# Adding C21 in place in PSUM, moving attention steps inside the periods, and another passage from the second to the third batch

## The chip, the cores and the metric

The kernel runs on 1 core of one Trainium2 chip. The metric is the device time of one execution in microseconds (us); lower is better. The engines are named as in the profile: PE (TensorE, matmuls; PEld its weight loads), DVE (VectorE), ACT (ScalarE), POOL (GpSimd) and SP (SyncE, which here only issues DMAs).

## The reference

Attention in two steps, then a gated feed-forward layer, in float32:

```python
def _attn_ref(q, k, v, p):                 # q, k, v: (8, 8, 576, 64); p: (8, 8, 32, 64)
    scale = 1.0 / np.sqrt(q.shape[-1])
    def sm_attn(qq, kk, vv):
        s = scale * np.matmul(qq, kk.transpose(0, 1, 3, 2))
        s = s - np.max(s, axis=-1, keepdims=True)
        a = np.exp(s)
        a = a / (np.sum(a, axis=-1, keepdims=True) + 1e-09)
        return np.matmul(a, vv)
    p_packed = sm_attn(p, k, v)            # 32 packed rows look at 576 keys
    return sm_attn(q, p_packed, p_packed)  # 576 rows look at the 32 packed rows

def _moe_ref(x, w_a, w_b, w_out):          # x: (4608, 512), w_a and w_b: (512, 1536), w_out: (1536, 512)
    return ((x @ w_a) * (x @ w_b) @ w_out).astype(np.float32)
```

`x` is the attention's output with the heads laid side by side: 8 batches of 576 rows.

## The kernel before

The kernel goes batch by batch (b = 0 to 7). `p_packed` is never multiplied into x. It is folded into the weights: for each batch and each of 12 column tiles `ft` of w_a and w_b, PE computes G = p_packed times the weights, and then a = A2 G, where A2 is the second attention's softmax. Every float32 product is made of three matmuls in a rounded format: the operand is split into a high part (a cast on ACT) and a low part (source minus high part: `lo_part`, L91, on POOL or DVE), and hi x hi, hi x lo and lo x hi are summed in PSUM. The last product (h times w_out, "mm2") is made in thirds of four `ft` each, tile of 128 rows by tile.

**Batches 0 and 1** multiply plainly (`mm1`, L383). After each half of an `ft` the function `between()` emits the steps written down for that slot in a string, `PLAN`, for the work on the next batch: 24 slots in the 12 `ft`, then one for each call of a loop in which PE makes 6 matmuls of mm2 per slot. What stands behind a ";" is emitted at the next making of G.

**Batches 2 to 7** save one product in eight by a scheme of seven products per `ft` (numbered 1 to 7 in `PRODUCTS`) on halves of 288 rows; two of their sums are kept apart as `d` and `c2` (C21). Each `ft` is a *period*, n = 0 to 71, and works on two `ft` at once: it ends tile n and begins tile n+1, in two pairs of PSUM banks, X and V, one bank of each for even and one for odd tiles. A period runs so:

- even n: `make_g(n + 2)`: PE L777 makes G for two tiles from weights `wr` that a DMA has brought (one buffer, asked for by `load_kept` as soon as the last pair has been read); ACT copies it (`gs`, L783, L785, L786); DVE and POOL make sums of its quarters (L788, L789, L792).
- products 5, 1 and 2; ACT copies X to `d` (L829); `split_h` casts the h of the period before (ACT L808) and POOL takes its low part; PE fills in mm2 matmuls (L720) as `FILLS` says; DVE adds V to `d` (L833).
- products 3 and 6, for which that copy must be done; ACT copies X to `c2` (L841); `split_g` casts a G tile (ACT L798) and POOL takes its low part; DVE makes the second half of h from X and `d` (L846).
- fill; products 4 and 7; DVE adds V to `c2` (L856) and multiplies by the `d` of the period before (L857); fill.

Between these parts `emit_steps` emits steps of the next batch's attention. Steps are names: "S0", "S1" begin the first attention for even and odd heads and "r0", "r1" go one yield further in it (`stage1`); "s0", "s1" go further in the second one (`stage2`: matmuls, a DVE transpose and maximum, a subtraction on POOL L323, the exponential on ACT L325, sums L328 to L330 on DVE, a product on POOL L331, a transpose on DVE L335); "P" and "T" turn a small tile on PE and copy it (`turned`, L242); "k" and "q" turn a loaded block on DVE (L124); "L.." issue DMAs on SP; "t" forms four differences of the softmax halves on POOL (`half_sums`, L598); "u0" to "u3" cast these to high parts on ACT (L612) and make their low parts on DVE (`half_parts`).

From L564 on the order is the order of the source on each engine: every engine works its own queue first in, first out, and an instruction that waits holds all behind it.

The **passage** from the second to the third batch: after the last `mm1`, PE has 96 matmuls of mm2 to fill in: 24 in the loop of slots, 36 in each of the periods n = -2 and n = -1, which start the scheme. Before the change all four `half_parts` stand between the loop and period -2:

```python
    for i in range(4):
        half_parts(NB, i)
```

Of the kernel before, what the change touches and what calls it, by code (L numbers as in the profile page):

```python
# [12 lines left out]
ALU = mybir.AluOpType  # L13
AX = mybir.AxisListType.X
# [5 lines left out]
def tile_packed_attn_gated_ffn(  # L20
# [35 lines left out]
    NB = 2  # L56
# [179 lines left out]
    def turned(dst, src, back=0):  # L236

        tp = bank_pair(True)[:, 0, :] if paired[0] else bank()
        cols = src.rearrange("p e d -> p (e d)")
        for i in range(2):  # L240
            nc.tensor.transpose(tp[:, P * i:P * i + P], cols[:, 64 * (i ^ back):64 * (i ^ back) + P], ident)
        nc.vector.tensor_copy(out=dst.rearrange("p i r j -> p (i r j)"), in_=tp[:, 0:2 * P])  # L242

    pp, paired, a2f_of = {}, [False], {}

    def stage1(b, e):
# [13 lines left out]
        nc.vector.tensor_reduce(out=nmx, in_=s, axis=AXY, op=ALU.max)  # L260
        nc.vector.tensor_scalar(out=nmx, in0=nmx, scalar1=-scale, scalar2=None, op0=ALU.mult)
        a1 = work(b, f"a1_{e}", [P, S], "t1")
        rs = sm.tile([P, 1], F32, name="rs")
# [43 lines left out]
    def stage2(b, e):  # L307
# [9 lines left out]
        s2 = work(b, f"s2_{e}", [P, TU, J], "t1")  # L317
        nc.vector.transpose(out=s2.rearrange("p (u x) j -> p u (x j)", u=2), in_=x[:, :, 0:HS])
        mx = sm.tile([P, TU], F32, name="mx")
        nc.vector.tensor_reduce(out=mx, in_=s2, axis=AX, op=ALU.max)  # L320
# [6 lines left out]
        sum2 = sm.tile([P, TU], F32, name="sum2")  # L327
        nc.vector.tensor_reduce(out=sum2, in_=s2, axis=AX, op=ALU.add)  # L328
        nc.vector.tensor_scalar(out=sum2, in0=sum2, scalar1=1e-9, scalar2=None, op0=ALU.add)
        nc.vector.reciprocal(out=sum2, in_=sum2)  # L330
# [121 lines left out]
    def emit(b, plan, tasks={}):  # L452

        for name in plan.split():
# [44 lines left out]

    PLAN = (" |  |  | S0 | r0 | r0 |  | r0 |  | r0 Lv1 ; S1 | r1 | q0 Lk2 | r1 | r1 |  | r1 q1 Lk3 Lv2 P0 |  | T2 | "  # L500
            "s0 s0 Lp4 | s0 s1 | s1 s0 | s0 s1 | s1 | s0 s1 k2 | s1 t | k3 | Lq2")
    PLAN = dict(enumerate(PLAN.split("|")))
# [113 lines left out]
    def emit_steps(b, steps):  # L616

        for name in steps.split():
            if name in "ABCD":
                emit(0, name)  # L620
            elif b >= B:
                continue
            elif name == "t":
                half_sums(b)
            elif name[0] == "u":
                half_parts(b, int(name[1]))
            else:
                emit(b, name)
# [126 lines left out]

    banks_of = {}

    def product(n, k, bank, first):
# [52 lines left out]
    def period(n, fills, steps):  # L811
# [5 lines left out]
        both = slice(0 if here and k0 == 0 or there and k1 == 0 else 1, 2 if here and k0 == 1 or there and k1 == 1 else 1)  # L817
        emit_steps(b + 1, steps[0])
        if more and n % 2 == 0:
            make_g(n + 2)  # L820
        emit_steps(b + 1, steps[1])
        if here:
# [4 lines left out]
        if here or there:  # L827
            d = d_of[n] = lp.tile([P, 2, HS], F32, name="d", bufs=2)
            nc.scalar.copy(out=d[:, both], in_=X[:, both, 0:HS])  # L829
        split_h(n - 1)  # L830
        fill(fills[0])
        if here or there:
            nc.vector.tensor_tensor(out=d[:, both], in0=V[:, both, 0:HS], in1=d[:, both], op=ALU.add)  # L833
        flush()
        emit_steps(b + 1, steps[2])
        if here:
            product(n, 3, X, False)
        if there:
            product(n + 1, 6, X, False)
            c2 = c2_of[n + 1] = lp.tile([P, HS], F32, name="c2", bufs=2)  # L840
            nc.scalar.copy(out=c2, in_=X[:, k1, 0:HS])  # L841
        if more:
            split_g(n + 2)
        if here:
            hf = hf_of[n] = sm.tile([P, 2, HS], F32, name="asb")
            nc.vector.tensor_tensor(out=hf[:, 1], in0=X[:, k0, 0:HS], in1=d[:, k0], op=ALU.mult)  # L846
        fill(fills[1])
        flush()
        emit_steps(b + 1, steps[3])
        if here:  # L850
# [3 lines left out]
        if here:  # L854
            c2 = c2_of.pop(n)
            nc.vector.tensor_tensor(out=c2, in0=V[:, k0, 0:HS], in1=c2, op=ALU.add)  # L856
            nc.vector.tensor_tensor(out=hf[:, 0], in0=d_of.pop(n - 1)[:, k0], in1=c2, op=ALU.mult)  # L857
        fill(fills[2])
        flush()
        emit_steps(b + 1, steps[4])  # L860

# [8 lines left out]
    filler[0] = block()  # L870
    while slot[0] <= max(plan) or (slot[0] - start) % 2:
        fill(6)
        flush()
        between()
    for i in range(4):
        half_parts(NB, i)
    STEPS = {0: ("S0", "", "r0", "r0 Lq1", "Lv1"), 1: ("", "", "r0", "", ""), 2: ("r0", "S1", "r1", "r1", ""),
# [65 lines left out]
```

## Time and profile before

| | |
|---|---|
| median of 3 runs | 739.31 us (738.4 to 740.46) |
| profiled execution, its own time | 738.6 us |
| its span, first to last instruction | 736.8 us |
| PE busy | 707.6 us (96%) |
| DVE, ACT, POOL busy | 474.8, 359.9, 424.6 us |
| mean granted PE clock | 0.995 |
| first period of batch 2; end of the last | about 207 us; about 714 us |

Read it so: PE is busy nearly always, so a change can only shorten the time by what PE still waits, or by the time in which it runs at a lower clock; the other engines count where PE waits for one of them. A row of a timeline is: start, duration, engine, line, operation, output <- input, shape, count, and in brackets the idle time of that engine before it and what ended it.

### The profile page before, as it was taken

The numbers are of one execution on the slowest core, as the hardware profiler recorded it, in microseconds if no ns is written. First come the engines' busy times: TensorE is split into PE (matmuls) and PEld (weight loads), VectorE is DVE, ScalarE is ACT, GpSimd is POOL, SyncE is SP. The second block draws the span as 40 slices with busy tenths as digits, with TensorE's granted clock in tenths as the row PEclk, the third lists the DMA queues.
The fourth block names the chain that finished last, engine by engine and source line by source line (L and its number), as shares of the span: only waits on it lengthen the run. The fifth ranks groups of instructions, "written<-read, shape, count | busy, mean of one in ns | idle before, by whom it ended". The sixth has DMA issues, their size and how long they took to land.

```text
span 736.8 us, 14156 instructions
## 1 busy us (share of the span) xinstructions
PE 707.6 (96%) x5558; PEld 574.3 (78%) x5558; DVE 474.8 (64%) x828; ACT 359.9 (49%) x724; POOL 424.6 (58%) x322
## 2 busy tenths in 40 slices
PE   6899999998899999999999999999999999999998
PEld 4488878886787876888788877778778887788886
DVE  3888655557255769676786668776686576755442
ACT  3787744543334455544554355553555445545420
POOL 0586752336234678656775568656685567856530
PEclk9999999999899999999999999999999999999999
DMA  8999954576234733555354564347235422224002
GB/s 253 381 248 293 256 102 90 180 196 214 68 90 141 175 120 90 157 156 142 109 118 116 139 171 112 90 135 195 87 90 143 138 86 70 102 79 151 1 1 72
DMA packets 177059, 102.37 MB, mean 139 GB/s; under 512 B 141280, under 2 KB 159456, under 8 KB 171616
## 3 DMA queue, kind: packets, MB, share of 16 engines
q1 hardware_dynamic: 176992, 101.47, 48.4%
q8 instruction: 43, 0.70, 0.4%
q14 instruction: 24, 0.20, 0.1%
HBM read 85.72 MB, written 15.73 MB: 138 GB/s over the span
## 4 chain that ended last, share of the span: by engine, by line
PE 75%; POOL 9%; DVE 5%; ACT 3%; DMA 3%; issue 3%; SPq 1%; DVEq 0%; POOLq 0%; ACTq 0%
PE x L720 30%; PE m L763 21%; PE m L383 8%; PE m L409 5%; PE x L777 4%; POOL G_lo L91 3%; DMA wr<-w_kept 2%; POOL h_lo L91 2%; POOL t L323 1%; PE s L298 1%; PE s L254 1%; PE s L313 1%; POOL t L331 1%; PE x L365 1%; ACT gs L783 1%
## 5 line engine op out<-in xcount | busy, mean ns | idle before, releaser
L720 PE MATMUL x<-wo,h_hi 128*128 128x512 f32 (+1 forms) x776 | 242.6, 392 | 5.9 <-ACT gs L783 5.6
L91 POOL TENSOR_TENSOR h_lo<-asb,h_hi 128x576 fp32r<-128x576 f32 x96 | 141.7, 1476 | 114.7 <-ACT h_hi L808 58.9
L720 PEld LDWEIGHTS x<-wo,h_hi 128*128 128x128 f32 x776 | 139.0, 189 | 27.2 <-ACT gs L783 8.0
L720 PE MATMUL x<-wo,h_lo 128*128 128x512 f32 (+1 forms) x388 | 152.1, 392 | 0.0
L91 POOL TENSOR_TENSOR G_lo<-gs,G_hi 128x640 fp32r<-128x640 f32 x72 | 114.2, 1586 | 47.5 <-ACT G_hi L798 47.5
L720 PEld LDWEIGHTS x<-wo,h_lo 128*128 128x128 f32 x388 | 73.2, 189 | 13.6
L833 DVE TENSOR_TENSOR d<-m,d 128x576 f32<-128x576 f32 (+1 forms) x73 | 54.3, 744 | 44.4 <-ACT d L829 44.2
L91 POOL TENSOR_TENSOR A_lo<-gs,A_hi 128x256 fp32r<-128x256 f32 x36 | 27.8, 773 | 77.3 <-ACT A_hi L786 77.3
L829 ACT COPY d<-m 128x576 f32<-128x576 f32 (+1 forms) x73 | 46.5, 637 | 52.0 <-PE m L763 35.2
L730 DVE TENSOR_TENSOR part<-x,part 128x512 f32<-128x512 f32 (+1 forms) x65 | 44.1, 679 | 36.3 <-PE x L720 36.2
L763 PE MATMUL m<-tx_hi,G_lo 128*128 128x288 f32 x216 | 63.8, 296 | 0.8 <-POOL G_lo L91 0.8
L763 PE MATMUL m<-tx_hi,G_hi 128*128 128x288 f32 x216 | 64.5, 299 | 0.0
L763 PE MATMUL m<-tx_lo,G_hi 128*128 128x288 f32 x216 | 63.5, 294 | 1.0 <-DVE tx_lo L91 1.0
L783 ACT COPY gs<-x 128x512 f32<-128x512 f32 x36 | 21.1, 587 | 87.7 <-PE x L777 73.0
L846 DVE TENSOR_TENSOR asb<-m,d 128x288 f32<-128x288 f32 x72 | 32.3, 449 | 45.4 <-ACT c L841 43.1
L763 PEld LDWEIGHTS m<-a_hi,G_hi 128*128 128x128 f32 x144 | 27.0, 187 | 43.7 <-issue 18.2
L857 DVE TENSOR_TENSOR asb<-d,c 128x288 f32<-128x288 f32 x72 | 58.0, 805 | 2.5
L798 ACT CAST G_hi<-gs 128x640 fp32r<-128x640 f32 x72 | 52.8, 733 | 13.0 <-POOL gs L792 13.0
L841 ACT COPY c<-m 128x288 f32<-128x288 f32 x72 | 28.8, 400 | 52.8 <-PE m L763 52.2
L763 PE MATMUL m<-a_hi,G_hi 128*128 128x288 f32 x144 | 48.7, 338 | 6.1 <-ACT d L829 6.0
L808 ACT CAST h_hi<-asb 128x576 fp32r<-128x576 f32 x72 | 49.3, 684 | 5.2 <-DVE asb L857 5.2
L792 POOL TENSOR_TENSOR gs<-gs 128x512 f32<-128x512 f32 x36 | 46.7, 1296 | 0.1
(169 smaller groups left out, 1560.2 us busy)
## 6 DMA issues: line engine op xcount, KB each, us to landing
wr<-w_kept SPq DMA_DIRECT2D x36, 1024.0 KB
nat<-in_k_dram SPq DMA_DIRECT2D x56, 144.0 KB
nat<-in_q_dram SPq DMA_DIRECT2D x56, 144.0 KB
vt<-in_v_dram SPq DMA_DIRECT2D x28, 256.0 KB
out_dram<-part SPq DMA_DIRECT2D x27, 256.0 KB
raw<-in_moe_w_a_dram SPq DMA_DIRECT2D x12, 512.0 KB
raw<-in_moe_w_b_dram SPq DMA_DIRECT2D x12, 512.0 KB
raw<-in_moe_w_out_dram SPq DMA_DIRECT2D x12, 512.0 KB
```

The costliest lines, as they stand in the source:

```text
L91: return eng.tensor_tensor(out=dst, in0=src, in1=hi.bitcast(F32), op=ALU.subtract)
L383: nc.tensor.matmul(out=ps[:, half, 0:HS], lhsT=gt[:, kt, ft % 4, cols], rhs=at[:, kt, HS * half:HS * half + HS], start=(n == 0 and kt == 0 ...
L409: nc.tensor.matmul(out=o[:, cols], lhsT=ht[:, c0:c0 + P], rhs=wt[:, cols], start=(ft == 0 and n == 0), stop=(ft == NFT - 1 and n == 2))
L720: nc.tensor.matmul(out=o[:, cols], lhsT=ht[:, c0:c0 + P], rhs=wt[:, cols], start=(ft == fts[0] and n == 0), stop=end)
L730: nc.vector.tensor_tensor(out=parts[i][:, cols], in0=o[:, cols], in1=parts[i][:, cols], op=ALU.add)
L763: nc.tensor.matmul(out=bank[:, n % 2, 0:HS], lhsT=g, rhs=t, start=(first and i == 0), stop=(i == 2), skip_group_check=True)
L792: nc.gpsimd.tensor_tensor(out=gs[:, 2:4].rearrange("p a u f -> p a (u f)"), in0=gs[:, 0:2].rearrange("p a u f -> p a (u f)"), in1=s2.unsqu ...
L798: nc.scalar.copy(out=G_hi[:, n % 3], in_=gs[:, 1:6, n % 2])
L808: nc.scalar.copy(out=view(h_hi[ft]), in_=src)
L829: nc.scalar.copy(out=d[:, both], in_=X[:, both, 0:HS])
L833: nc.vector.tensor_tensor(out=d[:, both], in0=V[:, both, 0:HS], in1=d[:, both], op=ALU.add)
L857: nc.vector.tensor_tensor(out=hf[:, 0], in0=d_of.pop(n - 1)[:, k0], in1=c2, op=ALU.mult)
```

## The change

It adds and removes no arithmetic. In words:

1. `c2` is added to V in place in PSUM (L856 writes V, no longer `c2`), and the product behind it (L857) reads V from PSUM and `d` from SBUF, where both of its inputs were in SBUF.
2. For batches 3 to 7 the row sums of the second softmax are written to 18 free columns of X's banks and read from there (L328, L329).
3. `stage1` and `stage2` get one more yield each for batches 3 to 7, so that maximum and exponential, and transpose and maximum, can stand at different places.
4. In odd periods `split_g` stands at the period's start, ahead of the copy to `d`; in even ones where it was. `split_h` stands after the first fill, no longer before it.
5. The steps of the attention are given new places (`STEPS`, with places named pre, post, a, b, c, end).
6. In the passage, the steps of the third batch's attention go further in earlier slots of `PLAN`; "u0" and "u1" stand in its slots 24 and 26, "u2" and "u3" inside period -2.
7. The copies of "P" and "T" go to ACT, from the passage on.

```diff
-        nc.vector.tensor_copy(out=dst.rearrange("p i r j -> p (i r j)"), in_=tp[:, 0:2 * P])
+        copy = nc.scalar.copy if paired[0] else nc.vector.tensor_copy
+        copy(out=dst.rearrange("p i r j -> p (i r j)"), in_=tp[:, 0:2 * P])
...
         nc.vector.tensor_scalar(out=nmx, in0=nmx, scalar1=-scale, scalar2=None, op0=ALU.mult)
+        if b > NB:
+            yield
...
         nc.vector.transpose(out=s2.rearrange("p (u x) j -> p u (x j)", u=2), in_=x[:, :, 0:HS])
+        if b > NB:
+            yield
...
-        nc.vector.tensor_reduce(out=sum2, in_=s2, axis=AX, op=ALU.add)
-        nc.vector.tensor_scalar(out=sum2, in0=sum2, scalar1=1e-9, scalar2=None, op0=ALU.add)
+        total = banks_of["x"][:, e, HS:HS + TU] if b > NB else sum2
+        nc.vector.tensor_reduce(out=total, in_=s2, axis=AX, op=ALU.add)
+        nc.vector.tensor_scalar(out=sum2, in0=total, scalar1=1e-9, scalar2=None, op0=ALU.add)
...
-    PLAN = (" |  |  | S0 | r0 | r0 |  | r0 |  | r0 Lv1 ; S1 | r1 | q0 Lk2 | r1 | r1 |  | r1 q1 Lk3 Lv2 P0 |  | T2 | "
-            "s0 s0 Lp4 | s0 s1 | s1 s0 | s0 s1 | s1 | s0 s1 k2 | s1 t | k3 | Lq2")
+    PLAN = (" |  |  | S0 | r0 | r0 |  | r0 |  | r0 Lv1 ; S1 | r1 | r1 q0 Lk2 | r1 | r1 | q1 Lk3 Lv2 P0 |  ; s0 | s0 s0 | s0 T2 | "
+            "s0 Lp4 | s0 s1 | s1 s1 | s1 | s1 | s1 | t u0 | k2 | u1 | k3 Lq2")
...
-        emit_steps(b + 1, steps[0])
+        step = lambda at: emit_steps(b + 1, steps.get(at, ""))
+        step("pre")
         if more and n % 2 == 0:
             make_g(n + 2)
-        emit_steps(b + 1, steps[1])
+        elif more:
+            split_g(n + 2)
+        step("post")
...                                         # products 5, 1, 2; the copy to d
-        split_h(n - 1)
         fill(fills[0])
...                                         # the sum d
         flush()
-        emit_steps(b + 1, steps[2])
+        step("a")
+        split_h(n - 1)
...                                         # products 3, 6; the copy to c2
-        if more:
+        if more and n % 2 == 0:
             split_g(n + 2)
...                                         # the second half of h (L846)
+        step("b")
         fill(fills[1])
         flush()
-        emit_steps(b + 1, steps[3])
+        step("c")
...                                         # products 4, 7
             c2 = c2_of.pop(n)
-            nc.vector.tensor_tensor(out=c2, in0=V[:, k0, 0:HS], in1=c2, op=ALU.add)
-            nc.vector.tensor_tensor(out=hf[:, 0], in0=d_of.pop(n - 1)[:, k0], in1=c2, op=ALU.mult)
+            v = V[:, k0, 0:HS]
+            nc.vector.tensor_tensor(out=v, in0=v, in1=c2, op=ALU.add)
+            nc.vector.tensor_tensor(out=hf[:, 0], in0=v, in1=d_of.pop(n - 1)[:, k0], op=ALU.mult)
         fill(fills[2])
         flush()
-        emit_steps(b + 1, steps[4])
+        step("end")
...
-    while slot[0] <= max(plan) or (slot[0] - start) % 2:
+    while slot[0] <= max(plan) or (slot[0] - start) % 4:
         fill(6)
         flush()
         between()
-    for i in range(4):
-        half_parts(NB, i)
-    STEPS = {0: ("S0", "", "r0", "r0 Lq1", "Lv1"), 1: ("", "", "r0", "", ""), 2: ("r0", "S1", "r1", "r1", ""),
-             3: ("", "", "q0 r1", "", "Lk2"), 4: ("r1", "", "", "P0", ""), 5: ("", "", "q1", "T2", "Lv2 Lk3 Lp4"),
-             6: ("s0", "", "s0", "s0", "s0"), 7: ("", "", "s0", "s0", ""), 8: ("s1", "", "s1", "s1", "s1"),
-             9: ("", "", "s1 k2", "s1", "t"), 10: ("", "", "u0", "k3", "u1"), 11: ("", "", "u2", "", "u3 Lq2")}
+    STEPS = {-2: {"a": "u2", "c": "u3"}, 0: {"pre": "S0", "c": "Lq1", "end": "r0 Lv1"}, 1: {"a": "r0", "b": "r0 r0"},
+             2: {"pre": "r0", "post": "S1", "end": "r1"}, 3: {"a": "r1", "b": "r1 r1", "c": "q0", "end": "Lk2"},
+             4: {"pre": "r1", "c": "P0", "end": "q1"}, 5: {"b": "T2", "end": "Lv2 Lk3 Lp4"},
+             6: {"pre": "s0", "a": "s0", "end": "s0 s0"}, 7: {"a": "s0", "c": "s0", "end": "s0"},
+             8: {"pre": "s1", "a": "s1", "end": "s1 s1 k2"}, 9: {"a": "s1", "c": "s1", "end": "s1 t"},
+             10: {"a": "u0", "end": "u1"}, 11: {"a": "k3", "c": "u2", "end": "u3 Lq2"}}
...
-        period(n, (12, 12, 12), ("",) * 5)
+        period(n, (12, 12, 12), STEPS.get(n, {}))
```

More of the change, by code (lines that the diff above doesn't have):

```diff
@@ L241, in turned @@
             nc.tensor.transpose(tp[:, P * i:P * i + P], cols[:, 64 * (i ^ back):64 * (i ^ back) + P], ident)
-        nc.vector.tensor_copy(out=dst.rearrange("p i r j -> p (i r j)"), in_=tp[:, 0:2 * P])
-    pp, paired, a2f_of = {}, [False], {}
+        copy = nc.scalar.copy if paired[0] else nc.vector.tensor_copy
+        copy(out=dst.rearrange("p i r j -> p (i r j)"), in_=tp[:, 0:2 * P])
+    pp, paired, a2f_of, banks_of = {}, [False], {}, {}
     def stage1(b, e):
@@ L754, in fill @@
             next(filler[0], None)
-    banks_of = {}
     def product(n, k, bank, first):
```

## The prediction

> **What bounds the kernel now.** I read the page's busy times first, then stretches cut at the copies to `d`, so that each is one batch of 12 periods (2 to 6, then 7), then the chain of waits and the timelines where PE stood.
>
> ```profile
> PE 707.6 (96%) x5558; PEld 574.3 (78%) x5558; DVE 474.8 (64%) x828; ACT 359.9 (49%) x724; POOL 424.6 (58%) x322
> ...
> 209.30:295.50 86.20, 83.60 (x665) 67.71 (x665) 62.00 (x111) 42.16 (x90) 55.85 (x43) 1.00 0.49 132
> 295.50:381.50 86.00, 85.24 (x676) 69.78 (x675) 61.31 (x111) 43.27 (x92) 57.36 (x44) 1.00 0.47 129
> 381.50:468.20 86.70, 83.94 (x664) 67.37 (x664) 62.08 (x111) 42.74 (x91) 57.29 (x44) 1.00 0.49 131
> 468.20:554.30 86.10, 85.35 (x676) 69.86 (x675) 61.41 (x111) 43.35 (x92) 57.36 (x44) 1.00 0.47 128
> 554.30:639.40 85.10, 82.47 (x646) 66.87 (x645) 58.94 (x108) 42.67 (x91) 57.47 (x44) 1.00 0.33 104
> 639.40:709.20 69.80, 69.80 (x443) 59.34 (x442) 36.48 (x66) 31.26 (x62) 41.30 (x31) 1.00 0.20 76
> ```
>
> Columns: stretch, length, busy PE, PEld, DVE, ACT, POOL, PE clock, DMA. PE stands 2.60, 0.76, 2.76, 0.75 and 2.63 us in the five batches that carry attention for the next one, together 9.5, and nothing in the last. So the periods can give 9.5 us at most. Even batches lose more.
>
> The passage:
>
> ```profile
> 179.20:186.60 7.40, 1.85 (x17) 0.31 (x16) 6.94 (x10) 3.55 (x9) 4.54 (x6) 0.76 0.67 135
> 186.60:190.30 3.70, 3.69 (x10) 2.95 (x11) 1.54 (x5) 0.53 (x2) 1.99 (x2) 0.56 0.42 173
> ...
> 162.58 1.60 PE m L383 x12
> ...
> 179.70 1.35 PE L777 MATMUL x<-wr,ppT 64*32 64x512 f32 x12
> 186.61 1.22 PE L720 MATMUL x<-wo,h_hi 128*128 128x512 f32 x2 [5.55 <-ACT gs L783]
> ...
> 179.64 1.16 POOL L331 TENSOR_TENSOR t<-t,sum 128x576 f32<-128x576 f32 x1 [0.41 <-DVE sum L330]
> 181.75 0.79 POOL L598 TENSOR_TENSOR tf<-t,t 128x288 f32<-128x288 f32 x1 [0.95 <-DVE t L335]
> 183.49 0.88 POOL L598 TENSOR_TENSOR tf<-t,t 128x288 f32<-128x288 f32 x1
> 184.40 0.67 ACT L612 CAST tx_hi<-tf 128x576 fp32r<-128x576 f32 x1 [2.33 <-POOL tf L598]
> 185.98 0.57 ACT L783 COPY gs<-x 128x512 f32<-128x512 f32 x1
> ```
>
> PE stands 5.55 us: the bank that its next mm2 tile wants is free only after the copy to `gs`, which waits in ACT's queue behind the casts of `half_parts`, these for POOL's third difference, the differences for the softmax. Then the clock is low: 3.70 us at 0.56 are 3.70 x 0.44 = 1.6 us lost. Passage: 7.2 us. All PE loss that this change touches is 9.5 + 7.2 = 16.7 us; 739.3 - 16.7 = 722.6 is the floor.
>
> **The change part by part.**
>
> *Passage.* In the new slots stage 2 of the even heads is emitted three slots earlier, of the odd heads one, and nothing of it stands behind the even heads' product. A slot is 12 matmuls of `mm1`, 1.60 us in the chain's row. My estimate, walked through the queues: the odd heads' product (L331), now ahead of the last h's low part and free of the even heads', comes one slot earlier by its place and about two more by what no longer stands before it on POOL and DVE, at about 174.3 to 175.5 instead of 179.64; behind it the transpose on DVE (by 176.3) and the last low part on POOL, and the differences start at about 177.2 instead of 181.75. The first three took 184.40 - 181.75 = 2.65, so u1's cast ends about 180.5. A copy of an mm2 tile (as the `gs` copy, 0.57) stands behind it and frees the bank of the second half of G: 181.1, then `gs`: 181.7. PE resumes near 181.8 instead of 186.61: 4.8 us gained, a wait of some 2 us left. Ends: only one slot gained, 1.6; the whole wait gone, 5.55. u2 and u3 in period -2 lie beside 36 filler matmuls; if one came late, product 5 or 3 of period 0 would wait.
>
> The clock: PE's last matmul ended at 181.05. A mean of 0.76 over 7.40 us is 7.40 x 0.24 / 0.5 = 3.55 us at half clock, so it fell near 183.05, 2.0 us into the wait. I take it that it now stays up, since G's matmuls end later in the wait than before: gain 1.6, with 0 as the other end. The Trainium skill, "TensorE: Matmul & The Clock Gate", section "HAM oscillation — how this bites in real kernels", asks for no idle gap over about 3.4 us; by that rule the clock stays up and the sum stands. The trace saw it fall sooner, and by that the 1.6 us would be lost again: 727.6.
>
> *Exponential ahead of the copy to `d`.* Before, it is emitted at the end of periods 6 and 8:
>
> ```profile
> 272.43 1.37 POOL L323 TENSOR_TENSOR t<-t,mx 128x576 f32<-128x576 f32 x1
> ...
> 273.83 0.68 ACT L325 ACTIVATE t<-t 128x576 f32<-128x576 f32 x1 [1.61 <-POOL t L323]
> 274.42 0.62 ACT L829 COPY d<-m 128x576 f32<-128x576 f32 x1
> ...
> 275.10 0.40 PE L763 MATMUL m<-a_hi,G_hi 128*128 128x288 f32 x1 [0.92 <-ACT d L829]
> ...
> PE m L763 <- ACT d L829: 6.0, 10, 0.9
> ACT t L325 <- POOL t L323: 20.5, 13, 3.5
> ACT d L829 <- PE m L763: 35.2, 20, 3.3
> ACT gs L783 <- POOL G_lo L91: 14.7, 7, 2.1
> ```
>
> ACT waits for POOL's subtraction with the copy to `d` queued behind, and PE behind that. Now the exponential stands at "a" of periods 7 and 9, after the copy. The subtraction comes no sooner (POOL's queue ahead of it is the same), but only h's cast and `c2` stand behind it. These waits go: about 0.9 + 0.6 in an even batch, 0.6 in an odd. The sums, at "c", and the product then end about half a period later, but the odd-period `split_g` no longer stands before the differences. That early `split_g` also ends the 14.7 us that `gs` waited for G's low part. Its cast now precedes the copy to `d`, where ACT mostly idles for PE (35.2 us, 20 times): nothing. If that cover is gone it costs up to its 0.73 us (below).
>
> *C21.*
>
> ```profile
> L857 DVE TENSOR_TENSOR asb<-d,c 128x288 f32<-128x288 f32 x72 | 58.0, 805 | 2.5
> L846 DVE TENSOR_TENSOR asb<-m,d 128x288 f32<-128x288 f32 x72 | 32.3, 449 | 45.4 <-ACT c L841 43.1 <-issue 1.6 <-POOL h_lo L91 0.5
> L856 DVE TENSOR_TENSOR c<-m,c 128x288 f32<-128x288 f32 x72 | 32.2, 448 | 13.9 <-PE m L763 11.4
> ...
> L857 DVE TENSOR_TENSOR asb<-d,c x72: 457/602/1542, 214.4 to 714.8; 128x288 f32<-128x288 f32 x72
> L329 DVE TENSOR_SCALAR sum<-sum 128x18 f32<-128x18 f32 x16 | 10.0, 625 | 0.5
> ```
>
> L857 takes the form of L846: 805 - 449 = 0.36 us less, x 72 = 25.6 us of DVE. No row shows DVE writing PSUM: L856 stays at 448 by its own row, between 0.40 and 0.81 (the span of these rows). V is held through L857 too, 0.45 us longer: its next write is product 2 of the next period, at least products 7, 5 and 1 later, so hidden unless DVE is late by more than about 1 us. The ten sums of batches 3 to 7 drop by at most 0.6 each. All this is DVE time with PE busy elsewhere: nothing on the path but what follows.
>
> *Periods 10 and 11 of even batches.*
>
> ```profile
> 280.18 1.10 POOL L598 TENSOR_TENSOR tf<-t,t 128x288 f32<-128x288 f32 x1
> 285.01 1.29 POOL L792 TENSOR_TENSOR gs<-gs 128x512 f32<-128x512 f32 x1
> ...
> 284.74 1.36 DVE L124 STREAM_TRANSPOSE xT<-nat 128x1152 f32<-128x1152 f32 x1
> 288.54 1.51 DVE L91 TENSOR_TENSOR tx_lo<-tf,tx_hi 128x576 fp32r<-128x576 f32 x1
> ...
> 286.34 0.73 ACT L798 CAST G_hi<-gs 128x640 fp32r<-128x640 f32 x1 [2.78 <-POOL gs L792]
> 286.97 0.67 ACT L612 CAST tx_hi<-tf 128x576 fp32r<-128x576 f32 x1
> 288.10 0.64 ACT L829 COPY d<-m 128x576 f32<-128x576 f32 x1 [0.46 <-DVE asb L857]
> ...
> 290.10 0.40 PE L763 MATMUL m<-tx_lo,G_hi 128*128 128x288 f32 x1 [0.51 <-DVE tx_lo L91]
> ```
>
> Before, "k3" (1.36) and a long L857 push `tx_lo` to 288.54 and PE to 290.10. "k3" is now a period later and L857 short. What is late next is POOL: differences from about 279.6, L792 done by 285.4, then on ACT 0.73 + 0.67 + the next G's cast 0.73 before the copy to `d`: done about 288.2, PE's product 6 about 288.7. So 1.4 us are gained here, and a wait of about 1 us stays. With 0.6 from period 7 an even batch gains 2.0, an odd 0.75 (all it loses): 3 x 2.0 + 2 x 0.75 = 7.5. Ends: 2.0 in all (POOL's chain as late as now) and 9.5.
>
> *DMA.* No load is added.
>
> ```profile
> 430.87 8.45 SPq L700 DMA_DIRECT2D wr<-w_kept  x2
> ...
> 437.75 1.09 PE L777 MATMUL x<-wr,ppT 64*32 64x512 f32 x16 [0.47 <-DMA wr<-w_kept]
> ```
>
> This `wr` queues on SP behind the loads of period 5, which keep their place, and lands 6.9 us after its issue. Where PE comes 0.6 sooner it waits as much longer: -0.6 in batch 4 alone. The two copies per batch that go to ACT (busy 43 of 86 us) and the extra yields cost nothing; without ACT's slack a copy would hold what is behind it some 0.4 us.
>
> *Sum.* 4.8 + 1.6 + 7.5 - 0.6 = 13.3. The profiled execution took 738.6 (span 736.8 and 1.8 around it): 725.3. The median of the three is 0.7 higher: 726.0. I say 726.
>
> **The rivals.**
> 1. *POOL keeps the periods.* POOL is busy 56 of 86 us and its order around the differences hardly changes; with `split_g`'s cast in front the copy to `d` in period 11 is no earlier. Then the periods give 2.0: 739.3 - 6.4 + 0.6 - 2.0 = 731.5. Against: L857 and "k3" leave DVE's queue there.
> 2. *The passage stays slow:* one slot gained and the clock falls: 739.3 - 1.6 - 6.9 = 730.8. For: the third difference still gates u1 and u1 the bank.
> 3. *Sums in X's banks.* PE's next product 5 in that bank must wait for DVE's sum. The Trainium skill, "PSUM — Partial Sum Buffer", section "PSUM bank collisions raise a hardware error", says two engines may not use one bank at once, whatever the columns. Between them lie products 4 and 7 and G's matmuls (the 1.09 above), about 2 us; if DVE is later, ten waits of about 0.8: 734.
> 4. *Slower: the early cast holds the copy to `d`.* If in the 30 odd periods ACT is not idle there, each pays 0.73: 21.9 us, 739.3 - 13.3 + 21.9 = 748. It decides from 13.3 / 30 = 0.44 us per odd period. Against: ACT's 20 waits for PE ahead of that copy, 1.8 us each.
> 5. *No change*, what is won reappearing elsewhere: 739.
>
> **How the numbers follow.** Forecast (723 to 729) 0.60, rival 1 0.15, 2 0.10, 3 0.05, 4 0.06, 5 0.04. About 0.3% (2.2 us) is what a measurement here can tell from no change. Faster: 0.60 + 0.15 + 0.10 + 0.05 = 0.90; within: 0.04; slower: 0.06. The range goes from the floor, 722, to rival 1 with 1.5 us over it, 733, which takes in both bounds of the passage: 0.85 by the cases.
>
> **What would show it.** Right: L857 near 449 and even; PE's wait in the passage near 2 us and the granted clock at 1.00 there; no wait of L325 with the copy to `d` behind it; PE's idle time per attention batch near 0.6 to 1.5 us. Wrong: PE waiting for `d` in period 11 over 1.5 us, for DVE's sum, for V, or for `wr` in more batches than one.

## The result, and the profile after

The changed kernel took 720.12 us (median of 4, 719.3 to 721.31); the kernel before, on the same chip, 738.86 (median of 4). The ratio of the two is 0.9745, 95% interval 0.9722 to 0.9767: 18.7 us faster. The prediction said 726.0, 722 to 733: the direction was right, the gain was 6 us too small, and the time lies below the range. The profiled execution of the changed kernel took 721.31 us with a span of 719.5; its mean granted clock is 1.0 (0.995 before).

The page's busy times, and the same six batches in stretches from copy to `d` to copy to `d` (columns: stretch, length, busy PE, PEld, DVE, ACT, POOL, PE clock, DMA share, GB/s):

```profile
PE 699.4 (97%) x5558; PEld 573.8 (80%) x5558; DVE 443.8 (62%) x819; ACT 362.4 (50%) x733; POOL 418.5 (58%) x322
```

```profile
200.50:285.10 84.60, 82.60 (x665) 67.78 (x665) 56.19 (x109) 42.86 (x92) 54.61 (x43) 1.00 0.50 134
285.10:369.50 84.40, 84.40 (x676) 70.08 (x675) 56.39 (x109) 44.02 (x95) 56.14 (x44) 1.00 0.49 132
369.50:454.90 85.40, 82.45 (x664) 67.64 (x663) 56.37 (x109) 43.47 (x94) 56.00 (x44) 1.00 0.49 133
454.90:539.20 84.30, 84.30 (x676) 69.97 (x675) 56.28 (x109) 43.88 (x94) 56.12 (x44) 1.00 0.48 130
539.20:622.00 82.80, 81.47 (x645) 67.20 (x645) 54.18 (x107) 43.18 (x92) 56.03 (x44) 1.00 0.34 107
622.00:692.30 70.30, 70.04 (x443) 59.35 (x442) 33.67 (x66) 31.32 (x61) 41.10 (x31) 1.00 0.21 76
```

Read the second row against the one of before: the same 676 matmuls are busy for 84.40 us instead of 85.24, at the same clock. The work is the same; PE's "busy" time held 0.84 us of waiting that no idle row shows. One such place is in period 0 of batch 5, before and then after: the first matmul of product 3 starts 0.39 us after the one ahead of it, later 0.23, and the row ahead of it hides the difference.

```profile
472.41 0.39 PE L720 MATMUL x<-wo,h_lo 128*128 128x512 f32 x1
472.80 0.40 PE L763 MATMUL m<-a_hi,G_hi 128*128 128x288 f32 x1
```

```profile
459.06 0.40 PE L726 MATMUL x<-wo,h_lo 128*128 128x512 f32 x1
459.29 0.30 PE L767 MATMUL m<-a_hi,G_hi 128*128 128x288 f32 x1
```

The prediction's ceiling ("PE stands 0.75 in an odd batch, all it loses") was read from idle time, and this is why it was too low.

A measure that does not depend on what counts as busy is the time from one making of G to the next (the first row of L777, L781 after the change, in PE's timeline, one for two periods). Between batch 1's first `mm1` and the start of the passage, over the passage, and from period 0 of batch 2 to the last making of G, all in us:

| kernel (profiled execution) | batch 1 | passage | periods | median of its runs |
|---|---|---|---|---|
| before | 56.15 | 27.69 | 482.46 | 738.3 to 739.6 |
| changed | 54.58 | 21.62 | 473.92 | 720.12 |
| e1 passage alone | 54.58 | 21.62 | 482.09 | 731.01 |
| e2 all but the passage | 56.16 | 28.96 | 471.62 | 728.89 |
| e3 C21 back in SBUF | 54.58 | 21.62 | 477.68 | 726.74 |
| e4 sums back in SBUF | 54.58 | 21.62 | 472.01 | 720.29 |
| e5 `split_g` back in the middle | 54.58 | 21.60 | 479.12 | 726.20 |
| e6 C21 alone | 56.16 | 28.33 | 482.57 | 740.78 |
| e7 loads later | 54.58 | 21.62 | 471.16 | 720.35 |
| e9 loads later, `split_g` 11 late | 54.58 | 21.66 | 471.14 | 720.73 |
| e10 two slots as before | 55.36 | 21.62 | 473.09 | 722.69 |
| e11 exponential as before | 54.58 | 21.62 | 479.90 | 727.84 |
| e12 new places without the two edits | 54.58 | 21.60 | 486.04 | 732.17 |
| e13 cast of u1 first | 54.58 | 21.66 | 470.52 | 718.57 |

Each ratio below is to the kernel before in the same session of runs; its median differs by up to 1.3 us between the sessions, so differences of medians from different sessions are no finer than that. Of the profiled pair's 17.3 us, 1.57 came in batch 1, 6.07 in the passage and 8.54 in the periods; the other 1.20 came before batch 1, where the profiled executions of all these kernels differ by up to 2.6 us (its first `mm1` starts at 121.9 to 124.5) with no pattern by kernel.

Two periods at a time, the first period's number at the left, before and after, and e7 where the two differ by a transfer:

| periods | batch 5 (odd) before, after | batch 6 (even) before, after | batch 2 before, after, e7 |
|---|---|---|---|
| 0 | 13.75, 13.48 | 13.76, 13.48 | 13.79, 13.79, 13.79 |
| 2 | 14.09, 14.12 | 16.81, 16.85 | 16.82, 16.86, 16.86 |
| 4 | 13.52, 13.35 | 13.12, 13.12 | 13.52, 13.35, 13.35 |
| 6 | 15.54, 15.55 | 13.69, 12.83 | 13.70, 13.71, 12.83 |
| 8 | 13.18, 12.32 | 13.52, 12.32 | 13.50, 12.34, 12.32 |
| 10 | 16.00, 15.57 | 14.21, 14.21 | 14.98, 14.70, 14.71 |

Most of the periods' gain lies in 6 to 9, not in 10 and 11, where the prediction put it.

The passage in the changed kernel, as its timeline has it:

```profile
176.24 0.80 POOL L604 TENSOR_TENSOR tf<-t,t 128x288 f32<-128x288 f32 x1
176.48 1.06 PE L781 MATMUL x<-wr,ppT 64*32 64x512 f32 x8
177.07 0.67 ACT L618 CAST tx_hi<-tf 128x576 fp32r<-128x576 f32 x1 [2.60 <-POOL tf L604]
...
177.65 0.58 ACT L734 COPY part<-x 128x512 f32<-128x512 f32 x1
177.78 0.76 DVE L91 TENSOR_TENSOR tx_lo<-tf,tx_hi 128x576 fp32r<-128x576 f32 x1 [1.00 <-ACT tx_hi L618]
178.13 0.59 ACT L787 COPY gs<-x 128x512 f32<-128x512 f32 x1
178.28 1.06 PE L781 MATMUL x<-wr,ppT 64*32 64x512 f32 x8 [0.74 <-ACT part L734]
```

It is the chain that the prediction walked: third difference, u1's cast, a copy of an mm2 tile. It ends earlier than walked, and PE waits 0.74 us instead of 5.55. What was left as "some 2 us" is 0.74.

### The profile page after: what moved, and what is told of

The parts are those of the page before. It is cut to its first block, busy times and chain, and to the rows that moved or that the text cites. A ratio compares the mean times of both kernels' runs of the same rounds, so it can differ in the third digit from the quotient of the medians.

```text
span 719.5 us, 14180 instructions
## 1 busy us (share of the span) xinstructions
PE 699.4 (97%) x5558; PEld 573.8 (80%) x5558; DVE 443.8 (62%) x819; ACT 362.4 (50%) x733; POOL 418.5 (58%) x322
## 4 chain that ended last, share of the span: by engine, by line
PE 83%; DVE 5%; POOL 4%; DMA 3%; ACT 2%; issue 1%; SPq 1%; DVEq 0%; POOLq 0%; ACTq 0%
PE x L726 33%; PE m L767 26%; PE m L389 7%; PE m L415 5%; PE x L781 4%; DMA wr<-w_kept 2%; PE s L301 2%; POOL tf L604 1%; PE s L316 1%; PE s L255 1%; DVE tx_lo L91 1%; DMA raw<-in_moe_w_b_dram 1%; PE x L371 1%; PE s L291 1%; SPq L182 1%
## 5 line engine op out<-in xcount | busy, mean ns | idle before, releaser
L91 POOL TENSOR_TENSOR h_lo<-asb,h_hi 128x576 fp32r<-128x576 f32 x96 | 138.7, 1445 | 75.6 <-ACT h_hi L408 37.1
L767 PE MATMUL m<-tx_lo,G_hi 128*128 128x288 f32 x216 | 63.6, 294 | 0.7 <-DVE tx_lo L91 0.7
L767 PE MATMUL m<-tx_hi,G_hi 128*128 128x288 f32 x216 | 64.2, 297 | 0.0
L767 PE MATMUL m<-tx_hi,G_lo 128*128 128x288 f32 x216 | 63.7, 295 | 0.0
L767 PEld LDWEIGHTS m<-a_hi,G_hi 128*128 128x128 f32 x144 | 27.0, 187 | 36.4 <-issue 18.2
L767 PE MATMUL m<-a_hi,G_hi 128*128 128x288 f32 x144 | 46.5, 323 | 3.3 <-ACT d L836 3.3
L865 DVE TENSOR_TENSOR m<-m,c 128x288 f32<-128x288 f32 x72 | 33.3, 462 | 23.6 <-PE m L767 21.7
```

The costliest lines, as they stand in the source:

```text
L91: return eng.tensor_tensor(out=dst, in0=src, in1=hi.bitcast(F32), op=ALU.subtract)
L767: nc.tensor.matmul(out=bank[:, n % 2, 0:HS], lhsT=g, rhs=t, start=(first and i == 0), stop=(i == 2), skip_group_check=True)
L865: nc.vector.tensor_tensor(out=v, in0=v, in1=c2, op=ALU.add)
```

## The experiments

**Each half by itself.** e1 is the kernel before with the new `PLAN`, the loop's bound and u0 to u3 in their new places; e2 is the changed kernel with those lines as before.

> The kernel before with the new slots and the new passage alone (PLAN, u0 to u3); periods as before. Theory (the gains add up by place): the two traces differ by 6.1 us between the first G of the late batches and the next, and by 1.6 us in the slots before it that are not a DMA wait of batch 0, so about 7.7 us faster than before, near 731.2; PE's wait in the passage under 1 us, clock 1.00 there. Rival (the 1.6 us, like the 1.2 us of batch 0, are chance between executions): 6.1 faster, near 732.8. Rival (the slots only help with the new periods): under 4 us.

> The kernel after with the slots and the passage of before; periods new. Theory (adding up): 8.5 us faster than before, near 730.3, the passage's wait of 5.5 us and the low clock are back. Rival (the periods' gain seen in the traces is partly chance, and my 6.9 was right): 6.9, near 732.

e1: 731.01 (730.15 to 731.64), ratio 0.9902 (0.9885 to 0.9918): 7.3 us, as expected. e2: 728.89 (727.09 to 729.35), ratio 0.9867 (0.9852 to 0.9883): 9.4 us, 1 more than expected; in its profile the periods are 10.8 us shorter and the passage 1.27 longer. By the medians the halves give 7.3 + 9.4 = 16.7 of the 18.7 us, and e2's longer passage is most of what is missing. The periods are what the prediction had too small.

**The sums.**

```diff
-        total = banks_of["x"][:, e, HS:HS + TU] if b > NB else sum2
+        total = sum2
```

> The kernel after with the row sums of the second softmax kept in SBUF. Theory: ten small sums go from 0.18 to about 0.6 us on DVE, in odd periods with slack: within 0.5 us of the kernel after, 720 to 721. Rival (sums in X's bank held PE up a little): up to 1 us faster than the kernel after. Rival (the sum holds POOL's product and the chain behind it): 1 to 3 us slower.

720.29 (720.0 to 720.86), ratio 0.9757 (0.9742 to 0.9771): no difference from the changed kernel. The sums in X's banks neither gain nor cost; the rival that PE would wait there is out.

**C21, in three settings.** e3 takes it out of the changed kernel, e6 puts it alone into the kernel before.

```diff
-            v = V[:, k0, 0:HS]
-            nc.vector.tensor_tensor(out=v, in0=v, in1=c2, op=ALU.add)
-            nc.vector.tensor_tensor(out=hf[:, 0], in0=v, in1=d_of.pop(n - 1)[:, k0], op=ALU.mult)
+            nc.vector.tensor_tensor(out=c2, in0=V[:, k0, 0:HS], in1=c2, op=ALU.add)
+            nc.vector.tensor_tensor(out=hf[:, 0], in0=d_of.pop(n - 1)[:, k0], in1=c2, op=ALU.mult)
```

> The kernel after with C21 added in SBUF as before, all else new. Theory (the order of the steps carries the periods; the 25 us of DVE lie beside PE): within 1.5 us of the kernel after, near 721; the product L866 goes back to 0.46 to 1.5 us. Rival (the shorter product carries the periods, through the copy to d and the release of V): over 3 us slower than the kernel after, 724 or more.

> The kernel before with C21 added in place in PSUM and nothing else. With C21 back in SBUF the changed kernel was about 6 us slower, so the edit is worth something once the rest is there; is it by itself? Theory A (C21's product is on the path wherever the first cast of the next g ends early or late): the product falls from a mean of 805 ns to about 458 ns, 72 x 347 ns = 25 us of VectorE, and the copies to d behind it come earlier in most periods: 3 to 6 us, 732.5 to 735.5. Theory B (it pays only with the casts moved: in the kernel before the last thing that the copy to d waits for is the cast, not the product): 738, within 1 us of the kernel before, with the product at 458 ns and the wait of TensorE for the copy to d as long as it was. What the prediction said, nothing by itself, is B.

e3: 726.74 (724.56 to 729.47), ratio 0.9845 (0.9818 to 0.9872). The theory, within 1.5 us of the changed kernel, fell. About half of what e3 loses lies in period 11 of the even batches: PE's three waits there for the copy to `d` grow from 3.3 us in all (1.09 in batch 2) to 6.2 (2.10). Another 0.3 us goes in period 0 of each of the batches 3 to 6 (13.81 in batch 5, against 13.48 in the changed kernel). e6: 740.78 (738.98 to 742.71, 12 runs) against 739.61 (17 runs), ratio 1.0016 (1.0005 to 1.0027): alone the edit gains nothing. The product by itself, in the list of line L865 (e3), then of L866 (changed) and L858 (e6): duration in ns, least, median and longest.

```profile
L865 DVE TENSOR_TENSOR asb<-d,c x72: 457/916/1585, 204.8 to 701.2; 128x288 f32<-128x288 f32 x72
```

```profile
L866 DVE TENSOR_TENSOR asb<-m,d x72: 457/457/460, 204.9 to 698.0; 128x288 f32<-128x288 f32 x72
```

```profile
L858 DVE TENSOR_TENSOR asb<-m,d x72: 456/457/460, 216.4 to 717.5; 128x288 f32<-128x288 f32 x72
```

e6 takes as much off the product as the change does (DVE is busy 453.4 us in it, 474.8 before) and is not faster. Its waits say why: the product now reads V, and PE waits for it.

```profile
PE m L763 <- ACT d L829: 4.0, 8, 0.7
PE m L763 <- DVE asb L858: 3.6, 8, 0.9
```

Before, the first of these was 6.0 and the second not in the list: 2.0 us less for `d`, 3.6 more for V. In the changed kernel, where the casts and steps lie elsewhere, the wait for V is 0.3 us, once.

**The place of `split_g` in the odd periods**, e5 (back in the middle, C21 in place), and e12, which undoes both at once, so that of the periods' edits only the steps' places, the later `split_h` and the sums are left:

```diff
-        elif more:
-            split_g(n + 2)
...
-        if more and n % 2 == 0:
+        if more:
             split_g(n + 2)
```

> The changed kernel with the split of g in the odd periods back in the middle, in front of the copy to d; C21 in place, the sums in X's banks and the passage stay. Theory: the moved split is the larger part of the 10.5 us that the periods gained: 4 to 7 us come back, 724 to 727, with the waits of TensorE for the copy to d in periods 1, 3, 7 and 11 as they were before. Rival: C21 in place carries the periods, and the split's place is worth only its walk of period 7 (0.6 us in three batches) and of period 11: 721 to 723.

> The changed kernel with C21 back in SBUF and the odd periods' split of g back in the middle at once: what is left is the passage, the new places of the steps and the sums. Each of the two alone took back some 6 us (726.7 and 726.2). Theory (they are not worth that by themselves: the new places shorten periods 6 to 9 by 8 us and lengthen the stretch from period 10 to the next period 0, and these two edits keep that stretch short, each for its own part): without both the stretch is 3 us longer than with both in every even batch and 1 us in the odd ones, 730 to 734, no faster than the passage alone (731.0). Rival (C21 adds nothing, as in the kernel before, where it alone gave 740.8 against 739.6): 726 to 727.

e5: 726.20 (724.55 to 728.42), ratio 0.9825 (0.9803 to 0.9847): 6 us back. e12: 732.17 (730.06 to 734.03), ratio 0.9908 (0.989 to 0.9926): no faster than the passage alone, as the theory said. The stretch from period 10 to the next period 0 in batch 2 is 14.98 us before, 14.70 changed, 15.83 in e3, 16.74 in e5, 17.88 in e12. So the new places of the steps load period 10 and 11, and the two edits carry that load. But the waits alone do not make these lengths. From the timelines: in the changed kernel PE stands 1.09 + 0.23 = 1.32 us there, in e5 0.96 + 0.85 = 1.81, only 0.49 more, where the stretch is 2.04 longer.

```profile
280.18 0.41 PE L767 MATMUL m<-a_hi,G_hi 128*128 128x288 f32 x1 [0.96 <-ACT d L834]
...
281.82 0.40 PE L767 MATMUL m<-tx_lo,G_hi 128*128 128x288 f32 x1 [0.85 <-DVE tx_lo L91]
```

The stretches of e5 around these two rows, columns as above, show the rest:

```profile
269.80:278.20 8.40, 8.40 (x62) 6.93 (x62) 6.66 (x14) 3.34 (x8) 7.27 (x8) 1.00 0.75 188
278.20:283.20 5.00, 3.20 (x14) 2.28 (x13) 3.51 (x3) 3.22 (x6) 4.86 (x4) 0.91 0.09 15
283.20:286.50 3.30, 3.30 (x26) 2.62 (x33) 2.29 (x5) 1.31 (x4) 1.56 (x1) 0.63 0.00 0
286.50:290.00 3.50, 3.50 (x39) 2.41 (x24) 2.57 (x8) 2.28 (x5) 1.04 (x2) 1.00 0.32 89
```

The clock falls: 5.00 x 0.09 + 3.30 x 0.37 = 1.7 us lost, and 0.49 + 1.7 = 2.2 is about the stretch. The same product of period 11 (L767, tx_hi times G_hi) then takes 0.45 us in e5's timeline and 0.30 in the changed kernel's:

```profile
284.68 0.45 PE L767 MATMUL m<-tx_hi,G_hi 128*128 128x288 f32 x1
```

```profile
281.47 0.30 PE L767 MATMUL m<-tx_hi,G_hi 128*128 128x288 f32 x1
```

It fell in all three even batches of that execution (0.62 and 0.65 after the other two). In the runs the time follows the clock: e5 724.55 us at a mean clock of 1.0 and 728.42 at 0.993; e3 724.56 at 0.999 and 729.47 at 0.995. So what C21 in place and the moved `split_g` are worth in the changed kernel, some 6 us each, is part shorter waits and part a clock that stays up: the executions that kept their clock, 724.55 and 724.56 us, are 4.4 us above the changed kernel's median.

**The exponential** (on e4, with the sums in SBUF):

```diff
-             6: {"pre": "s0", "a": "s0", "end": "s0 s0"}, 7: {"a": "s0", "c": "s0", "end": "s0"},
-             8: {"pre": "s1", "a": "s1", "end": "s1 s1 k2"}, 9: {"a": "s1", "c": "s1", "end": "s1 t"},
+             6: {"pre": "s0", "a": "s0 s0", "c": "s0", "end": "s0"}, 7: {"a": "s0", "c": "s0"},
+             8: {"pre": "s1", "a": "s1 s1", "c": "s1", "end": "s1"}, 9: {"a": "s1 k2", "c": "s1", "end": "t"},
```

> The changed kernel with its sums in SBUF (720.3 by itself) and the steps of the second softmax in periods 6 to 9 where they were: subtraction at c, exponential at the end, ahead of the next copy to d. By the gaps between the makings of G, the pairs of periods 6-7 and 8-9 got shorter by 0.87 and 1.2 us in the even batches and 0 and 0.86 in the odd ones, with C21 in either place and the split of g in either place. Theory: it is the exponential's place that does this; back it costs 2.6 + 4.9 = 7.5 us: 727 to 728.5, with TensorE's waits for the copy to d in periods 7 and 9. Rival: the later cast of h (after the fill) or the kept sums give it: 720 to 722.

727.84 (726.9 to 728.63), ratio 0.985 (0.9837 to 0.9864): 7.5 us back, as expected. Its timeline has the scene of the kernel before again, ACT waiting for POOL's subtraction with a cast and the copy to `d` queued behind:

```profile
265.42 0.68 ACT L330 ACTIVATE t<-t 128x576 f32<-128x576 f32 x1 [1.02 <-POOL t L328]
266.01 0.71 ACT L802 CAST G_hi<-gs 128x640 fp32r<-128x640 f32 x1
266.63 0.63 ACT L836 COPY d<-m 128x576 f32<-128x576 f32 x1
...
267.31 0.41 PE L767 MATMUL m<-a_hi,G_hi 128*128 128x288 f32 x1 [0.95 <-ACT d L836]
```

In the changed kernel the copy goes first:

```profile
263.82 0.64 ACT L836 COPY d<-m 128x576 f32<-128x576 f32 x1
...
264.68 0.69 ACT L330 ACTIVATE t<-t 128x576 f32<-128x576 f32 x1 [0.21 <-POOL t L328]
```

PE's waits for the copy to `d`: 8.2 us in 10 in e11, 3.3 in 3 in the changed kernel, 6.0 in 10 before. Back in place the exponential costs 3.8 us in periods 6 and 7 and 6.0 in 8 and 9, over the five batches, and gives 2.0 back in 10 and 11, since the differences on POOL then start earlier: 7.9 by the traces. The edit moves the maximum, the subtraction, the sums and the last transpose of the second softmax together with the exponential; that the exponential is the one that counts is read from the waits of ACT and PE above, not from a run that moves it alone.

**The loads**, e7: "Lv2 Lk3 Lp4" at the end of period 6, behind the load of the kept weights.

```diff
-             4: {"pre": "r1", "c": "P0", "end": "q1"}, 5: {"b": "T2", "end": "Lv2 Lk3 Lp4"},
-             6: {"pre": "s0", "a": "s0", "end": "s0 s0"}, 7: {"a": "s0", "c": "s0", "end": "s0"},
+             4: {"pre": "r1", "c": "P0", "end": "q1"}, 5: {"b": "T2"},
+             6: {"pre": "s0", "a": "s0", "end": "s0 s0 Lv2 Lk3 Lp4"}, 7: {"a": "s0", "c": "s0", "end": "s0"},
```

> The changed kernel with the three loads for the next products issued at the end of period 6, behind the load of the kept weights, instead of at the end of period 5, ahead of it. Theory: the waits of TensorE for the kept weights in period 8 (1.07 us at 255.8 and 2.0 us at 425.6 in the changed kernel's profile, none in two of its variants) are a matter of which transfer the queues take first; with the order turned round they are gone in every execution: 719 to 720, and the executions lie closer together than the 2 us between the changed kernel's fastest and slowest. Rival: the transfers only change places, and the steps that use the three loads wait instead: 720 to 722.

720.35 (719.27 to 720.72), ratio 0.974 (0.9722 to 0.9758). The waits for `wr` in period 8 are gone: the changed kernel's timeline has

```profile
425.58 1.09 PE L781 MATMUL x<-wr,ppT 64*32 64x512 f32 x16 [1.63 <-DMA wr<-w_kept]
```

and e7 has at the same place

```profile
424.78 1.06 PE L781 MATMUL x<-wr,ppT 64*32 64x512 f32 x16
```

The periods are 2.76 us shorter than in the changed kernel's profile, but the medians are the same. What the trace says of one execution is confirmed, a gain in the median is not. One reason is that the wait differs between executions: with the loads where the change has them it is 2.3 us in the changed kernel's profile, 0.5 in e3's and e4's (by the lists of PE's waits), and the start differs too.

**Two slots of batch 1**, e10: P0 one slot earlier than in the changed kernel, right behind the first attention's last step again, and the first "s0" behind the pause that the making of G leaves PE, no longer in it. (The expectation calls the place of P0 "one slot later"; the edit moves it from slot 14 to slot 13.)

```diff
-    PLAN = (" ... | r1 | q1 Lk3 Lv2 P0 |  ; s0 | s0 s0 | s0 T2 | "
+    PLAN = (" ... | r1 P0 | q1 Lk3 Lv2 |  | s0 s0 s0 | s0 T2 | "
```

> The changed kernel with two places of batch 1's slots as they were: the turn P0 one slot later, right behind the first attention's last step, and the steps s0 after the making of G's pause as in the kernel before, no longer behind it. Theory: the 1.6 us by which the passage starts earlier (179.25 to 177.66 where only the passage was changed) come from these two: 0.6 us of a wait of TensorE behind P0 and 0.9 us behind the cast for G: 721.7, the start of the passage later by 1.5 us against its own batches 0 and 1. Rival: they come from the other new places (r1, the load Lp4): 720.2, no change.

722.69 (721.51 to 722.97), ratio 0.9776 (0.9762 to 0.9789). Batch 1 is 55.36 us long against 54.58: 0.78 of the 1.57 us, with the wait behind P0 back. The kernel before, then e10:

```profile
156.28 0.44 PE L241 MATMUL x<-ident,pp 128*128 128x128 f32 x2 [0.41 <-DVE pp L304]
```

```profile
153.27 0.44 PE L241 MATMUL x<-ident,pp 128*128 128x128 f32 x2 [0.41 <-DVE pp L307]
```

So half is shown by the run. The traces show where the other half lies. In the kernel before, P0 stands directly ahead of the making of G for tiles 9 to 11, whose second part then waits for the copy of P0's small tile, and this copy stands on DVE behind the transpose of "q1":

```profile
157.10 1.86 PE L365 MATMUL x<-w_ab,ppT 64*32 64x512 f32 x16
...
157.43 0.39 DVE L242 COPY ppT<-x 128x256 f32<-128x256 f32 x1
...
157.87 0.18 PEld L365 LDWEIGHTS x<-w_ab,ppT 64*32 64x32 f32 x14 [0.66 <-DVE ppT L242]
```

In e10, as in the changed kernel, mm1 matmuls stand between P0 and this G, and the same 16 matmuls take 0.80 us less. In e10:

```profile
157.29 1.06 PE L371 MATMUL x<-w_ab,ppT 64*32 64x512 f32 x16
```

No idle row of PE shows this wait either. Why the median rose by more than the trace's 0.78 is open.

**What holds period 11 now.** Both versions have the later loads and `split_g` of period 11 behind the copy to `d`; e13 also casts tx_hi (u1) ahead of G in period 10, with its low part at the period's end as before.

```diff
-        elif more:
+        elif more and n % NFT != NFT - 1:
             split_g(n + 2)
...
-        if more and n % 2 == 0:
+        late = n >= 0 and n % NFT == NFT - 2
+        if more and (n % 2 == 0 or n % NFT == NFT - 1) and not late:
             split_g(n + 2)
...
         step("b")
+        if more and late:
+            split_g(n + 2)
...
-              10: {"a": "u0", "end": "u1"}, 11: {"a": "k3", "c": "u2", "end": "u3 Lq2"}}
+              10: {"a": "u0", "b": "u1h", "end": "u1l"}, 11: {"a": "k3", "c": "u2", "end": "u3 Lq2"}}
```

> The changed kernel with the loads at the end of period 6 and, in period 11 alone, the split of g back behind the copy to d. In the changed kernel's period 11 the first cast of the even batches waits 3.13 us for VectorE's and GpSimd's sums of g, and the copy to d stands behind two casts (276.17 to 278.01), so TensorE waits 1.09 us for it at 278.69. Theory: with the copy ahead of the casts this wait goes in the even batches, and the casts still end before the next period's products: 3 x 1 us below the kernel with the later loads, 716 to 718. Rival: the casts come too late for the first products of period 0, which then wait as long: 719 to 722.

> The changed kernel with the loads of period 5 at the end of period 6, in period 11 the split of g behind the copy to d, and in period 10 the cast of u1 (tx_hi) ahead of the cast of g, its low part at the period's end as before. In the kernel with the first two alone TensorE still waits 0.47 us for the copy to d and 0.86 us for the low part tx_lo in period 11 of an even batch, 1.33 together against 1.09 + 0.23 in the changed kernel: the cast of tx_hi stands in ScalarE's queue behind that of g, which waits 3.13 us for GpSimd, though its source is ready 2 us earlier. Theory: both waits go, 1.3 us in three batches, 4 us in all: 716 to 717.5. Rival: the low part runs beside GpSimd's work longer still (2.08 us instead of 1.5), or a copy of mm2's tile now waits behind the cast: 719.5 to 722.

The changed kernel, e9 and e13, each with the waits of period 11 of batch 2:

```profile
278.69 0.40 PE L767 MATMUL m<-a_hi,G_hi 128*128 128x288 f32 x1 [1.09 <-ACT d L836]
...
279.71 0.40 PE L767 MATMUL m<-tx_lo,G_hi 128*128 128x288 f32 x1 [0.23 <-DVE tx_lo L91]
```

```profile
279.67 0.40 PE L767 MATMUL m<-a_hi,G_hi 128*128 128x288 f32 x1 [0.47 <-ACT d L836]
...
281.32 0.40 PE L767 MATMUL m<-tx_lo,G_hi 128*128 128x288 f32 x1 [0.86 <-DVE tx_lo L91]
```

```profile
273.74 0.40 PE L767 MATMUL m<-tx_hi,G_hi 128*128 128x288 f32 x1 [0.26 <-ACT tx_hi L618]
...
279.39 0.40 PE L767 MATMUL m<-tx_hi,G_lo 128*128 128x288 f32 x1 [0.81 <-POOL G_lo L91]
```

The wait goes from `d` to tx_lo to G's low part, and stays about as long (1.32, 1.33, and 0.81 after a new 0.26 in period 10). e9: 720.73 (719.48 to 721.79), ratio 0.9748 (0.9729 to 0.9767), no gain: the rival held. e13: 718.57 (718.32 to 719.27), ratio 0.9727 (0.9714 to 0.9739): the theory's 4 us did not come, only 0.2 in each even batch by the trace. e13 is the fastest version run, though its interval overlaps that of the changed kernel. What stands behind all three waits is POOL with its chain of differences, sums of g and low parts: G's low part is made by it, and tx_lo runs beside it. That POOL holds period 11 whatever the order on ACT is argued from these rows; no run shortened its chain.

## Why the prediction was wrong

**The 6 us by parts.** The profiled execution took 721.31 us where 725.3 was forecast for it. Of these 4.0 us, about 1.6 are the slots of batch 1, 1.6 the periods (8.54 against 7.5 - 0.6) and 1.2 a start that came earlier for no reason that was found; the passage gave 0.3 less. The other 1.9 us are chance of the executions that were profiled: the median was forecast 0.7 above the profiled execution and came 1.2 below it.

**Passage and clock: right.** 6.4 predicted, 6.07 measured, by the chain that was walked. The clock stayed at 1.00. The Trainium skill's rule that was weighed there ("TensorE: Matmul & The Clock Gate", section "HAM oscillation — how this bites in real kernels"), no idle gap over about 3.4 us, was not put to the test by a wait of 0.74. e5 speaks against it, where the clock fell with no wait over 0.96 us.

**Slots of batch 1: costed at nothing, 1.57 measured.** The prediction looked at the new `PLAN` only for when the passage's chain starts, not for where PE waits inside batch 1: 0.8 us at the making of G behind P0, the rest at P0 itself and in the pause that "s0" now fills.

**Periods: the step that failed is "an even batch gains 2.0, an odd 0.75 (all it loses)", 7.5 in all; 10.5 measured with 0.5 us of waits for the weights (e4), 11.3 with none (e7), 8.5 in the changed kernel's profile with 2.3.** Its parts:
- *The exponential* was named rightly, with 0.9 + 0.6 in an even batch and 0.6 in an odd one, but only the 0.6 of period 7 went into the even batch's sum. Measured: 0.86 + 1.20 = 2.06 in batch 6, 0.86 in batch 5. Over the five batches the sum has 5 x 0.6 = 3.0, and taking it back costs 7.9 (e11). This is the largest error.
- *Periods 10 and 11*: 1.4 in an even batch was predicted, 0.28 came in batch 2 and nothing in batch 6. The step that failed is that tx_lo, the low part that "u1" makes, would be early because "k3" and the long product leave DVE's queue. It does start earlier: 277.58 is 9.42 us after period 10's making of G, before it was 10.28. But it ran 2.08 us instead of 1.51, so it ended only 0.29 earlier:

```profile
277.52 3.57 POOL L91 TENSOR_TENSOR G_lo<-gs,G_hi 128x640 fp32r<-128x640 f32 x2
277.58 2.08 DVE L91 TENSOR_TENSOR tx_lo<-tf,tx_hi 128x576 fp32r<-128x576 f32 x1 [1.83 <-POOL h_lo L91]
```

  In the passage the same tx_lo took 0.76. Rival 1, "POOL keeps the periods", fits these two periods, and these alone.
- *The ceiling.* Idle time of PE was taken as all that can be won; the small stalls of periods 0, 4 and 10 (0.27, 0.17 and 0.43 in an odd batch) lay for the most part in busy time. Period 0's gain goes with C21 in place (e3 does not have it); period 4's stands in every version with the new places of the steps, and whether the places give it or the copies of "P" and "T" on ACT was not separated. The floor of 722.6 built on the ceiling was no floor, and the range ended there.

**C21: "nothing on the path but what follows"** holds in the kernel before (e6) and fails in the changed one (e3, 6.6 us by the medians). The prediction priced each edit by itself against the trace of before; the one that moves work into periods 10 and 11 also makes DVE's time there count.

**The kept weights: -0.6 in batch 4.** The wait there grew from 0.47 to 1.63 us in the changed kernel's profile, and a new one of 0.68 came in batch 2; e7 has neither. The sign was right, and a single -0.6 too little for that execution; the size differs between executions.

**The signs.** The product at 457 ns, the clock and an exponential with no copy to `d` behind it came as named. PE's idle time did not lie at 0.6 to 1.5 us per batch (2.0, 2.95 and 1.33 in the even batches, 0 in the odd ones), and PE waited for `wr` in two batches, which had been named as a sign of being wrong.

**Rivals 2 to 5 did not come:** PE waits 0.74 in the passage; the sums cost nothing (e4); the early cast does hold the copy to `d` in period 11 of even batches, but taking it away gains nothing (e9); the time changed.

## What to carry to other kernels

Idle time of the busiest engine is no ceiling for what a reordering can give: compare the busy time of the same number of instructions, and lengths between fixed marks, before a floor is set on it. An edit that only frees an engine off the path is worth nothing alone and much together with the one that loads that engine, so price the edits in the schedule that they make, not in the old one. When a wait moves from one releaser to the next at the same length, look for the engine behind all of them.

## What the runs showed of the hardware

- *The clock fell on short waits.* In e5 two waits, 0.96 and 0.85 us, with 0.8 us of matmuls between them, were followed by a granted clock of 0.63 over 3.3 us; in e3 waits of 2.10 and 0.21 us in the same place were not (1.00 from 276 to 283.1 in its profile), though other executions of it ran at 0.995. The Trainium skill, "TensorE: Matmul & The Clock Gate", section "What's actually happening", says that the activity window runs freely, not in step with the kernel; that one kernel's executions differ in clock, from 0.992 to 0.999 in e12, agrees with it. So does e12's profile: waits of 1.48 and 0.83 us stand in period 11 of all three even batches, and the clock fell to 0.53 and 0.57 behind two of them and stayed at 1.00 behind the third. What decides was not isolated.
- *DVE beside POOL.* A DVE instruction with two inputs in SBUF varies with what POOL does (product 457 to 1585 ns in e3, where all that ran beside no POOL instruction took 457 to 460; tx_lo 0.76 to 2.12 us), one with an input in PSUM does not (456 to 460). The Trainium skill, "SBUF — State Buffer", section "Who interferes with whom", says that the first kind contends with a GpSimd instruction that reads SBUF and the second does not; these runs agree, and they give the price.
- *DVE writing PSUM in place* took 467 ns in the median for 128x288 (431 to 467, L865), against 457 (408 to 458, L856 before) into SBUF.
